# Two decode layers on one core: gate and up sums turned by VectorE, two query pieces ahead of the first query

## The chip, the cores and the metric

The kernel runs on one core of one Trainium2 chip. The metric is the device time of one execution in microseconds (us), lower is better; it was run three times. A separate execution was profiled. Engines are named TensorE (PE; its weight loads are listed apart as PEld), VectorE (DVE), ScalarE (ACT), GpSimd (POOL) and SyncE (SP), which here only issues DMA transfers.

## The reference

One token for each of two batch rows goes through attention, a gated feed-forward, the same attention and the same feed-forward again, with the same weights and the same caches both times:

```python
def _A_ref(x, k_cache, v_cache, wq, wo):          # x (2,1,576), caches (2,32,8192,128)
    q = (x @ wq).reshape(B, Sq, H, Dh).transpose(0, 2, 1, 3)
    scores = jnp.einsum("bhqd,bhkd->bhqk", q, k_cache) * (Dh ** -0.5)
    p = _softmax(scores, axis=-1)
    o = jnp.einsum("bhqk,bhkd->bhqd", p, v_cache)
    return o.transpose(0, 2, 1, 3).reshape(B, Sq, H * Dh) @ wo

def _B_ref(x, w_gate, w_up, w_down):              # 576 -> 4608 -> 576
    h = _gelu(x @ w_gate) * (x @ w_up)
    return h @ w_down

x = A_x
x = x + _A_ref(_layernorm(x), ...)
x = x + _B_ref(_layernorm(x), ...)
x = x + _A_ref(_layernorm(x), ...)
x = x + _B_ref(_layernorm(x), ...)
```

Everything is float32. The caches together are 537 MB and are read twice, less some pieces that are kept on the chip.

## The kernel before

**Space.** One SBUF tile, `space`, holds everything that comes from HBM: 49,920 floats in each partition. The class `Space` keeps a hand-written list of transfers in the order in which SyncE issues them. Each has a place, fixed or taken from a ring, and goes out when the place is free: `done(key)` after the last use of a piece frees its place, and `pump` issues what then fits. SyncE issues strictly in this order, so a transfer that waits for its place holds up all behind it. In the end the wait is on the reads of just those columns that the new transfer overwrites. Attention's key and value pieces use three large places of eight parts (a part is 2048 floats in each partition). Everything between the two attentions (output weights, the first feed-forward's weights, the second attention's query weights) goes through one ring, `mid`, of 6912 floats in each partition.

**Attention** (`attention`). The work is cut into items: a batch row with two heads (30 of them) or, for the last two heads, with one (4). For each item VectorE multiplies the keys by the query (L529), GpSimd adds halves of the products (L533), VectorE sums the rest (L539), then come a maximum (L550, a transposition on TensorE L552, L557), the exponent on ScalarE, and the values' products on TensorE (L601). The second attention takes the items backwards and starts with keys that stayed in SBUF. Its query weights arrive in pieces named `("wq", 1, half, i, s)`; `first_of_queries` multiplies those of the second half of the heads into `acc[1]`, `rest_of_queries` those of the first half into `xps`, and both stand on TensorE behind the first query (`query(0)`, L501), since the first items need only the tail of the query weights (`("wq", 1, "t")`).

**The normalization.** The sums are made from the raw x, beside a third column that sums the weights themselves; `norm` then makes `rstd` and `shift`, and a 6-row sum becomes the normalized result when its rows are weighted with `rstd` and `shift`. `pick`, `spread` and `chosen` are these weights, laid out so that a product on TensorE applies them: `chosen` in `query`, `spread` in `turned`.

**Feed-forward** (`mlp`). Gate and up sums of one half of the 4608 columns are collected in two PSUM banks (`products`, L719), 6 rows in each group of 32 partitions: three for gate, three for up. They have to get from rows to columns, since the down product needs the hidden values along the partitions. `copy` takes the banks to SBUF (`o`; ScalarE L729, VectorE L730), `turned` makes the columns with small products on TensorE that apply `spread` at the same time (L749 in layer 0: 72 for each half; L740 in layer 1: 18 for each half), and `gelu` works on the result (L758 to L764). A float32 product shows as two rows in the profile. `lower` multiplies with a piece of the down weights (L771); a quarter t of the rows uses half t // 2. In layer 0, `turned(0)` and `gelu(0)` stand among the products of the second half, and `turned(1)` and `gelu(1)` behind the first piece of the down weights. In layer 1, both halves are turned after the last up product.

Of the kernel before, what the change touches and what calls it, by code (L numbers as in the profile page):

```python
# [9 lines left out]
F32 = mybir.dt.float32  # L10
# [5 lines left out]
P = 128  # L16
# [81 lines left out]
def decode_layers(ctx, tc, x_in, kc, vc, wq, wo, wg, wu, wd, out):  # L98
# [202 lines left out]
    for c in range(4):  # L301
# [18 lines left out]
    pick = consts.tile([P, 4, 2, RW], F32, name="pick")  # L320
    nc.vector.tensor_copy(
        pick.rearrange("p c g r -> p c (g r)"), ident.rearrange("p (c x) -> p c x", c=4)[:, :, 0:WIN]
    )
# [27 lines left out]
    spread = consts.tile([P, 8, B], F32, name="spread")  # L351
# [39 lines left out]
    def norm(apart):  # L391
# [4 lines left out]
        for b in range(B):  # L396
# [3 lines left out]
        rstd = work.tile([P, B], F32, name="rstd")  # L400
        nc.gpsimd.tensor_tensor(out=rstd, in0=ve, in1=mhalf, op=ALU.pow)  # L401
        shift = work.tile([P, B], F32, name="shift")
        nc.vector.scalar_tensor_tensor(shift, mv[:, :, 0], -1.0, rstd, op0=ALU.mult, op1=ALU.mult)
        k8 = pick.rearrange("p c g r -> p (c g) r")
        part = work.tile([P, 8, B], F32, name="part")
        nc.vector.tensor_mul(spread, k8[:, :, 0:B], rstd.unsqueeze(1).to_broadcast([P, 8, B]))
        nc.vector.tensor_mul(
            part, k8[:, :, B:RW].to_broadcast([P, 8, B]), shift.unsqueeze(1).to_broadcast([P, 8, B])
        )
        nc.vector.tensor_add(spread, spread, part)  # L410
        nc.vector.reduce_sum(
            chosen.rearrange("p g b -> p (g b)"), spread.rearrange("p (c g) b -> p (g b) c", c=4), axis=AX.X
        )
# [9 lines left out]
    def attention(layer, items, apart):  # L423
# [35 lines left out]

        def first_of_queries():  # L460
            for i in range(NW):
                for s in range(2):
                    queries(
                        acc[1], window(1, i), at_of["wq", 1, 1, i, s], i == s == 0, False, s, range(4 - s)
                    )
                    done(("wq", 1, 1, i, s))
# [181 lines left out]

        query(0)
# [61 lines left out]
    def mlp(layer, apart):  # L711
# [3 lines left out]
        def products(half, s, lhs, at, stop):  # L715
            for c in range(4):
                key = half, s, c
                lo = at + (c * CF + s * BF if layer else c * BF)
                nc.tensor.matmul(  # L719
                    banks[half][s][32 * c:32 * c + WIN, 0:BF], lhs, space[:, lo:lo + BF],  # L720
                    start=key not in done_first, stop=stop,
                )
                done_first.add(key)

        o, gu, ga, hT = {}, {}, {}, {}

        def copy(half):
            t = o[half] = once.tile([P, 2, BF], F32, name="o", tag="row")
            nc.scalar.activation(t[:, 0, :], banks[half][0][:, 0:BF], AF.Copy)  # L729
            nc.vector.tensor_copy(t[:, 1, :], banks[half][1][:, 0:BF])  # L730

        def turned(half):
            t = o[half]
            gu[half] = psum2.tile([P, NI, 2, 2, B], F32, name="gu", tag="small")
            if layer:
                t = t.rearrange("p s w -> p (s w)")
                sel = spread.rearrange("p (c e g) b -> p e c g b", c=2, e=2)
                for i in range(NI):
                    for e in range(2):
                        nc.tensor.matmul(  # L740
                            gu[half][HALF * e:HALF * e + HALF, i, :, :, :], t[:, i::NI], sel[:, e, :, :, :],
                            start=True, stop=True,
                        )
                return
            sel = spread.rearrange("p (c g) b -> p c g b", c=4)
            for s in range(2):
                for i in range(NI):
                    for c in range(4):
                        nc.tensor.matmul(  # L749
                            gu[half][32 * c:32 * c + 32, i, s, :, :], t[:, s, i::NI], sel[:, c, :, :],  # L750
                            start=True, stop=True,
                        )

        def gelu(half):
            g = once.tile([P, NI, 2, B], F32, name="g")
            a = once.tile([P, NI, 2, B], F32, name="a")
            hT[half] = work.tile([P, NI, 2, B], F32, name="hT")
            nc.vector.tensor_copy(g, gu[half][:, :, :, 0, :])  # L758
# [5 lines left out]
            nc.vector.scalar_tensor_tensor(hT[half], a, 0.5, gu[half][:, :, :, 1, :], op0=ALU.mult, op1=ALU.mult)  # L764

        def lower(t, lo, hi):
            at = at_of["d", layer, t, lo]
            for i in range(lo, hi):
                for c in range(4):
                    a = at + (i - lo) * D + c * CW  # L770
                    nc.tensor.matmul(  # L771
                        xps[32 * c:32 * c + B, 0:CW], hT[t // 2][:, i, t % 2, :], space[:, a:a + CW],
# [4 lines left out]
        if layer == 0:  # L777
            for half in range(2):
                for g, name in enumerate("gu"):
                    for i in range(NW):  # L780
# [12 lines left out]
                copy(half)  # L793
            d = downs[0]
            lower(*d[0])
            turned(1)
            gelu(1)
            for piece in d[1:]:
                lower(*piece)
        else:  # L800
            def several(name, g, off, n):
                for u in range(off, off + n):
                    at = at_of[name, 1, off] + (u - off) * HF
                    for s in range(2):
                        products(u % 2, s, window(g, u // 2), at, u >= 6 and g == 1)
# [5 lines left out]
            for half in range(2):  # L811
                for s in range(2):
                    products(half, s, both, at_of["m", 1, half], False)
# [46 lines left out]
```

## Time and profile before

| | |
|---|---|
| median of 3 runs | 2699.47 us (2699.2 to 2701.33) |
| profiled execution | 2698.3 us, of which the span of the instructions 2696.5 us |
| instructions | 19594 |
| busy: PE, DVE, POOL, ACT | 952.5 (35%), 1870.6 (69%), 1171.5 (43%), 93.5 (3%) us |
| moved by DMA | 1154.45 MB, mean 428 GB/s |

How to read the lines further down. In a timeline a row is a run of instructions of one line: start in us, length in us, engine, line, operation, output<-inputs, shapes, count, and in brackets how long the engine stood before it and what released it. In a table of stretches a row is the stretch, its length, the busy time of PE, PEld, DVE, ACT and POOL with counts, the granted TensorE clock as a share of full speed, the mean busy share of the 16 DMA engines, and GB/s. In groups a row ends with busy us, mean ns of one | idle us before them. A DMA issue stands under SPq; its length is that of the issue and not of the transfer.

### The profile page before, as it was taken

To read this page: it belongs to the slowest core of one execution; us is meant where nothing else is said; L and a number is where in the kernel's file an instruction comes from. 1 tells how busy PE (TensorE), PEld (TensorE's weight loads), DVE (VectorE), ACT (ScalarE), POOL (GpSimd) and SP (SyncE) were. 2 spreads that over 40 slices of the span, in tenths; PEclk is the share of its full clock that TensorE was granted. 3 is DMA by queue.
4 is the path that set the end of the run, shared out by engine and by line. 5 is a ranking of instruction groups with operands and counts; after the bars stand their busy time and mean duration, and the time that the engine had idled before them with its cause. 6 is when DMAs were issued, how large, how long until landed. Compare 5 with 4: busy or idle time off the path is not lost.

```text
span 2696.5 us, 19594 instructions
## 1 busy us (share of the span) xinstructions
PE 952.5 (35%) x8132; PEld 343.0 (13%) x8132; DVE 1870.6 (69%) x1330; ACT 93.5 (3%) x421; POOL 1171.5 (43%) x342
## 2 busy tenths in 40 slices
PE   1332332233233323335664233233223322332346
PEld 0110111011111100112121011011101110110023
DVE  4678777877777777787048777877687778667750
ACT  0000000000000000000000000000000000000000
POOL 2445444544554455454025544544454445445530
PEclk7656665666566566656676665666566656665677
DMA  9999999999999999999999999999999999999998
GB/s 420 434 434 433 435 428 435 434 431 435 432 429 435 431 435 435 432 428 411 410 365 435 432 435 434 433 433 430 434 434 432 434 435 431 432 430 435 433 426 375
DMA packets 37226, 1154.45 MB, mean 428 GB/s; under 512 B 4225, under 2 KB 4881, under 8 KB 16145
## 3 DMA queue, kind: packets, MB, share of 16 engines
q1 hardware_dynamic: 37112, 1153.19, 99.6%
q8 instruction: 64, 1.05, 0.2%
q14 instruction: 26, 0.20, 0.0%
q10 hardware_dynamic: 24, 0.01, 0.0%
HBM read 1153.18 MB, written 0.00 MB: 428 GB/s over the span
## 4 chain that ended last, share of the span: by engine, by line
DMA 20%; DVE 15%; PE 9%; POOL 7%; issue 4%; ACT 1%; POOLq 0%; DVEq 0%; SPq 0%
DMA space<-in_A_k_cache_dram 17%; DVE space L529 9%; POOL space L533 7%; PE acc L601 6%; DVE S L539 5%; DMA space<-in_B_w_down_dram 2%; DMA space<-in_B_w_up_dram 1%; DVE osb L617 1%; PE nb L560 1%; ACT prz L572 1%; DMA space<-in_A_wq_dram 1%; PE xps L640 0%; PE tot L582 0%; DMA space<-in_A_wo_dram 0%; PE mT L552 0%
## 5 line engine op out<-in xcount | busy, mean ns | idle before, releaser
L533 POOL TENSOR_TENSOR space<-space 128x2048 f32<-128x2048 f32 (+1 forms) x332 | 1168.0, 3526 | 1302.3 <-DVE space L529 1025.7
L529 DVE TENSOR_TENSOR space<-space,qp 128x4096 f32<-128x4096 f32 (+1 forms) x332 | 1136.0, 3437 | 465.7 <-DMA space<-in_A_k_cache_dram 465.0
L539 DVE TENSOR_REDUCE S<-space 128x32 f32<-128x2048 f32 (+1 forms) x332 | 595.6, 1794 | 115.8 <-POOL space L533 112.9
L601 PE MATMUL acc<-space,prz 128*8 128x512 f32 x4096 | 590.4, 739 | 0.6 <-DMA space<-in_A_v_cache_dram 0.6
L625 PE MATMUL po<-weights,osb 128*32 128x1 f32 x1024 | 59.6, 201 | 1145.2 <-DVE osb L617 1145.2
L625 PEld LDWEIGHTS po<-weights,osb 128*32 128x32 f32 x1024 | 54.1, 154 | 1163.3 <-DVE osb L617 1163.1
L552 PE MATMUL mT<-ident,m 128*1 128x128 f32 x68 | 25.2, 370 | 406.6 <-DVE m L550 406.6
L601 PEld LDWEIGHTS acc<-space,prz 128*8 128x8 f32 x4096 | 112.4, 103 | 413.4 <-issue 409.7
L630 ACT COPY oT<-po 64x4 f32<-64x4 f32 (+1 forms) x68 | 10.7, 157 | 1905.0 <-PE po L625 1905.0
L617 DVE SCALAR_TENSOR_TENSOR osb<-acc,diag,osb 128x128 f32<-128x128 f32 x204 | 71.6, 351 | 7.2
L401 POOL TENSOR_TENSOR rstd<-ve,mhalf 128x2 f32<-128x2 f32 x4 | 2.8, 698 | 162.8 <-DVE ve L399 162.8
L560 PE MATMUL nb<-m,strip 1*128 1x1 f32 x256 | 64.7, 351 | 22.7 <-DVE m L557 22.7
L560 PEld LDWEIGHTS nb<-m,strip 1*128 1x128 f32 x256 | 58.9, 314 | 41.2 <-DVE m L557 41.1
L582 PE MATMUL tot<-rs,strip 128*128 128x2 f32 x120 | 34.9, 361 | 77.3 <-ACT prz L572 77.3
L552 PEld LDWEIGHTS mT<-ident,m 128*1 128x1 f32 x68 | 5.4, 79 | 418.6 <-DVE m L550 371.8
L572 ACT ACTIVATE prz<-S,nbs 64x128 f32<-64x128 f32 (+1 forms) x136 | 53.3, 392 | 3.3 <-ACT nbs L568 0.2
L557 DVE TENSOR_REDUCE m<-mT 1x2 f32<-1x128 f32 (+1 forms) x68 | 18.9, 278 | 34.3 <-PE mT L552 34.3
L582 PEld LDWEIGHTS tot<-rs,strip 128*128 128x128 f32 x120 | 29.8, 308 | 82.5 <-ACT prz L572 82.5
L719 PE MATMUL acc<-space,xt 128*6 128x288 f32 x256 | 30.4, 592 | 27.2 <-DMA space<-in_B_w_up_dram 14.9
L730 DVE COPY o<-acc 128x288 f32<-128x288 f32 x2 | 0.9, 458 | 52.4 <-PE acc L719 52.4
L615 DVE TENSOR_SCALAR osb<-acc,diag 128x128 f32<-128x128 f32 x68 | 23.3, 342 | 19.1 <-PE acc L601 19.1
L771 PE MATMUL xps<-space,hT 128*2 128x144 f32 x576 | 28.3, 356 | 13.6 <-DMA space<-in_B_w_down_dram 11.5
(93 smaller groups left out, 329.8 us busy)
## 6 DMA issues: line engine op xcount, KB each, us to landing
space<-in_A_k_cache_dram SPq DMA_DIRECT2D x6, 4096.0 KB, 21.4
space<-in_A_v_cache_dram SPq DMA_DIRECT2D x3, 4096.0 KB, 27.2
space<-in_B_w_gate_dram SPq DMA_DIRECT2D x18, 576.0 KB, 8.1
space<-in_B_w_up_dram SPq DMA_DIRECT2D x18, 576.0 KB, 7.8
space<-in_A_wo_dram SPq DMA_DIRECT2D x16, 576.0 KB, 7.1
space<-in_A_wo_dram SPq DMA_DIRECT2D x8, 1152.0 KB, 29.0
space<-in_B_w_gate_dram SPq DMA_DIRECT2D x2, 4608.0 KB
space<-in_B_w_down_dram SPq DMA_DIRECT2D x3, 2592.0 KB, 44.0
```

Of the source, the lines that this page charges most:

```text
L529: nc.vector.tensor_tensor(out=u, in0=t, in1=qp[n % 2][:, 0:DH].unsqueeze(1).to_broadcast([P, j, DH]), op=ALU.mult)
L533: nc.gpsimd.tensor_tensor(out=half, in0=half, in1=u[:, :, DH // 2:], op=ALU.add)
L539: nc.vector.tensor_reduce(out=S[n][:, 16 * lo:16 * hi], in_=half, axis=AX.X, op=ALU.add)
L552: nc.tensor.transpose(peaks[n], m, ident)
L560: nc.tensor.matmul(low[n], one_of[e] if heads == 2 else ones[0:1, :], m1[:, e:e + 1], start=(e == 0), stop=(e == heads - 1),)
L572: nc.scalar.activation(prz[rows_, n % 2, 0:item.rows // 4, e, :], s[rows_, 0:item.rows].rearrange("p (g r) -> p g r", r=4), AF.Exp, bias=n ...
L582: nc.tensor.matmul(tot, ones, rs[:, n % 2, :], start=True, stop=True)
L601: nc.tensor.matmul(acc[n % 2][32 * c:32 * c + 8, :], prz[:, n % 2, g, :, :].rearrange("p e r -> p (e r)"), space[:, at:at + 4 * DH], start ...
L617: nc.vector.scalar_tensor_tensor(t, q[:, r, :], diag[:, r:r + 1], t, op0=ALU.mult, op1=ALU.add)
L625: nc.tensor.matmul(po[lo + 32 * e:lo + 32 * e + 32, n % 2, i:i + 1], t[:, i::GH], w[:, e:e + 1], start=True, stop=True,)
L719: nc.tensor.matmul(banks[half][s][32 * c:32 * c + WIN, 0:BF], lhs, space[:, lo:lo + BF], start=key not in done_first, stop=stop,)
L771: nc.tensor.matmul(xps[32 * c:32 * c + B, 0:CW], hT[t // 2][:, i, t % 2, :], space[:, a:a + CW], start=(t == 0 and i == 0), stop=(t == NT ...
```

## The change

1. `copy`, `turned` and `gelu` become `hidden`. VectorE turns each PSUM bank in 32x32 blocks straight into SBUF (`nc.vector.transpose`, 128x288, read in steps of nine columns), and three further VectorE operations apply `rstd` and `shift`. The turning products, the ScalarE copies and `spread` are gone; `rstd` and `shift` become lasting tiles. `hidden(half)` stands directly behind the half's last sum in both layers, and all `lower` follow.
2. `chosen` is made directly, in three VectorE operations in place of four, from a smaller `pick`.
3. In the second attention the first two pieces of the query weights (`body(0)`, 7 products) are multiplied ahead of `query(0)`.
4. In layer 1 the columns of a half are cut in another order between the two banks, with the same number of products. The four output transfers are dealt differently to the two queues, still two for each.

The order and the waits of all transfers into SBUF stay the same.

```diff
-    pick = consts.tile([P, 4, 2, RW], F32, name="pick")
-    nc.vector.tensor_copy(...)
+    pick = consts.tile([P, 2, RW], F32, name="pick")
+    nc.vector.reduce_sum(pick.rearrange("p g r -> p (g r)"), blocks[:, 0:WIN, :], axis=AX.X)
...
-        nc.vector.tensor_mul(spread, k8[:, :, 0:B], rstd.unsqueeze(1).to_broadcast([P, 8, B]))
...
-        nc.vector.tensor_add(spread, spread, part)
-        nc.vector.reduce_sum(
-            chosen.rearrange("p g b -> p (g b)"), spread.rearrange("p (c g) b -> p (g b) c", c=4), axis=AX.X
-        )
+        nc.vector.tensor_mul(chosen, pick[:, :, 0:B], rstd.unsqueeze(1).to_broadcast([P, 2, B]))
...
+        nc.vector.tensor_add(chosen, chosen, part)
...
+        def body(i):
+            for s in range(2):
+                queries(acc[1], window(1, i), at_of["wq", 1, 1, i, s], i == s == 0, False, s, range(4 - s))
+                done(("wq", 1, 1, i, s))
+
         def first_of_queries():
-            for i in range(NW):
-                for s in range(2):
...
+            for i in range(1, NW):
+                body(i)
...
+        if layer == 1:
+            body(0)
         query(0)
...
-                lo = at + (c * CF + s * BF if layer else c * BF)
+                lo = at + c * BF
...
+        def hidden(half):
+            t = once.tile([P, 2, NI, 32], F32, name="turned", tag="row")
             for s in range(2):
...
+                nc.vector.transpose(t[:, s, :, :], banks[half][s][:, 0:BF].rearrange("p (j k) -> p k j", k=NI))
+            rows_ = t.rearrange("p s k w -> p (s k) w")[:, :, 0:WIN].rearrange("p t (g r) -> p t g r", g=2)
+            shape = [P, 2 * NI, 2, B]
+            gu = once.tile(shape, F32, name="gu")
+            part = once.tile(shape, F32, name="gupart")
+            nc.vector.tensor_mul(gu, rows_[:, :, :, 0:B], rstd.unsqueeze(1).unsqueeze(1).to_broadcast(shape))
+            nc.vector.tensor_mul(
+                part, rows_[:, :, :, B:RW].to_broadcast(shape), shift.unsqueeze(1).unsqueeze(1).to_broadcast(shape)
+            )
+            nc.vector.tensor_add(gu, gu, part)
+            g, u = gu[:, :, 0, :], gu[:, :, 1, :]
...
-                        if half == 1 and g == i == 0:
-                            turned(0)
-                            gelu(0)
...
-                copy(half)
-            d = downs[0]
-            lower(*d[0])
-            turned(1)
-            gelu(1)
-            for piece in d[1:]:
-                lower(*piece)
+                hidden(half)
...
             for half in range(2):
-                copy(half)
-                turned(half)
-                gelu(half)
-            for piece in downs[1]:
-                lower(*piece)
+                hidden(half)
+        for piece in downs[layer]:
+            lower(*piece)
```

More of the change, by code (lines that the diff above doesn't have):

```diff
@@ L723, in products @@
                 done_first.add(key)
[L725 to L745, printed above, removed]
-            for s in range(2):
[L747 to L752, printed above, removed]
@@ L812, in mlp @@
                 for s in range(2):
-                    products(half, s, both, at_of["m", 1, half], False)
+                    products(half, s, both, at_of["m", 1, half] + s * CF * 2, False)
                 done(("m", 1, half))
```

40 lines of the change are left out of this document (15 added, 25 removed).

## The prediction

> **What bounds the kernel now.** I read the page first, for the busy shares and the transfer rate along the span.
>
> ```profile
> span 2696.5 us, 19594 instructions
> ...
> DMA  9999999999999999999999999999999999999998
> GB/s 420 434 434 433 435 428 435 434 431 435 432 429 435 431 435 435 432 428 411 410 365 435 432 435 434 433 433 430 434 434 432 434 435 431 432 430 435 433 426 375
> ...
> q8 instruction: 64, 1.05, 0.2%
> ```
>
> No compute engine is over 69%, the DMA engines are full in nearly every slice, and the rate stands at 428 to 435 GB/s except around slices 19 to 21 and at the end. A slice is 2696.5 / 40 = 67.4 us, so the dip lies at about 1213 to 1415 us: the output weights, the first feed-forward layer and the query weights of the second attention, which all go through one small ring of SBUF. So I asked for the rate by stretches.
>
> ```profile
> 20.00:1180.00 1160.00, 360.87 (x2685) 124.41 (x2681) 840.33 (x526) 38.40 (x174) 532.12 (x147) 0.61 1.00 433
> ...
> 1300.00:1340.00 40.00, 27.26 (x372) 5.90 (x368) 2.03 (x10) 0.64 (x2) 0.00 (x0) 0.74 1.02 411
> 1340.00:1353.00 13.00, 10.33 (x234) 4.68 (x230) 1.62 (x7) 0.64 (x2) 0.00 (x0) 0.53 1.02 408
> 1353.00:1364.00 11.00, 4.73 (x93) 2.67 (x91) 0.00 (x0) 0.00 (x0) 0.00 (x0) 0.78 0.82 276
> 1364.00:1373.00 9.00, 6.62 (x108) 3.01 (x112) 0.00 (x0) 0.00 (x0) 0.00 (x0) 0.53 1.02 417
> 1373.00:1383.00 10.00, 7.25 (x77) 2.77 (x70) 4.47 (x18) 0.38 (x1) 0.69 (x1) 0.84 1.00 365
> 1383.00:1392.00 9.00, 5.49 (x69) 1.79 (x62) 8.71 (x6) 0.00 (x0) 6.68 (x3) 0.88 0.84 269
> 1392.00:1490.00 98.00, 52.26 (x347) 17.56 (x341) 78.68 (x70) 6.45 (x30) 49.28 (x19) 0.67 1.02 431
> 1490.00:2600.00 1110.00, 345.14 (x2552) 119.82 (x2552) 827.63 (x521) 36.81 (x169) 525.80 (x144) 0.61 1.00 433
> ```
>
> The last three columns are the granted TensorE clock, the DMA share and GB/s. Transfers are the bound: both long attention stretches run at 433 GB/s with a DMA share of 1.00. The engines go short in two places only, at 1353 to 1364 (share 0.82, 276 GB/s) and at 1383 to 1392 (0.84, 269 GB/s). A microsecond of transfer won there moves everything behind it, because 1392 to 2600 has no hole to swallow it.
>
> What the holes cost: the first has the layer's gate and up rate of 411 GB/s as its measure, 11 x (1 - 276/411) = 3.6 us. The second has as measures the 365 just ahead of it, with many small rows, giving 9 x (1 - 269/365) = 2.4 us, and 411, giving 3.1 us; I take the middle, 2.7. Together 6.3 us, bounds 6.0 to 6.7.
>
> **First hole: the products that turn the sums.** TensorE around it, then SyncE's issues of the down weights, with their row of the table of transfers as the last line (count, KB each, median us from issue to landing):
>
> ```profile
> 1345.34 1.15 PE L719 MATMUL qp<-space,xm 128*6 128x288 f32 x8 [0.27 <-DMA space<-in_B_w_up_dram]
> 1347.45 1.62 PE L771 MATMUL xps<-space,hT 128*2 128x144 f32 x24 [0.97 <-DMA space<-in_B_w_down_dram]
> 1348.85 2.39 PE L749 MATMUL gu<-spread,o 128*32 128x4 f32 x144
> 1351.08 2.10 PE L771 MATMUL xps<-space,hT 128*2 128x144 f32 x30
> 1355.14 3.88 PE L771 MATMUL xps<-space,hT 128*2 128x144 f32 x74 [1.97 <-issue]
> 1360.44 0.67 PE L771 MATMUL xps<-space,hT 128*2 128x144 f32 x16 [1.42 <-DMA space<-in_B_w_down_dram]
> ```
>
> ```profile
> 1349.13 0.33 SPq L189 DMA_DIRECT2D space<-in_B_w_down_dram  x1
> ...
> 1352.28 0.33 SPq L189 DMA_DIRECT2D space<-in_B_w_down_dram  x1
> ...
> 1355.81 0.33 SPq L189 DMA_DIRECT2D space<-in_B_w_down_dram  x1
> ...
> space<-in_B_w_down_dram SPq DMA_DIRECT2D x12, 576.0 KB, 7.4
> ```
>
> The first down piece is multiplied at 1347.45, then 144 turning products (L749) hold TensorE for 2.39 us, and then it stands 1.97 us with "issue" as its releaser. The ring holds 6912 floats a partition, 3.54 MB, or 8.6 us at 411 GB/s; a piece takes 7.4 us from issue to landing and some 1.15 us of TensorE. The loop of 8.55 us has no room for a delay of 2.39 + 1.97 = 4.4 us. The issues show it: after 1349.13 the next two, which need the second and third piece's room, come at 1352.28 and 1355.81.
>
> Afterwards the products are gone from TensorE (the order of its instructions shows the down products in one unbroken run of 144), and VectorE does two block turns from PSUM and three small operations instead. The down products of the first two quarters need only the first half's result, long ready, so TensorE takes the second piece at 1347.45 + 1.62 = 1349.1 and the third by about 1350.3. The two issues then come at about 1350.2 and 1351.4, 2 and 4.4 us earlier, which is before the engines run dry. The stretch 1364 to 1373 is the same loop without turning products: 417 GB/s. So the hole closes: **-3.6 us**, bounds -2.0 (if the "issue" wait stays, below) and -3.6. The first half's products (another 144) delayed no transfer: 1300 to 1340 is at 411. They count nothing.
>
> **What VectorE's new work costs.** The nearest rows:
>
> ```profile
> L373 DVE STREAM_TRANSPOSE xt<-x 128x128 f32<-128x128 f32 x4 | 1.6, 405 | 0.1
> ...
> L385 DVE STREAM_TRANSPOSE xtm<-x 128x32 f32<-128x32 f32 x4 | 0.9, 235 | 0.1
> ...
> L730 DVE COPY o<-qp 128x288 f32<-128x288 f32 x2 | 0.9, 454 | 19.9 <-PE qp L719 19.9
> ...
> L759 DVE TENSOR_TENSOR a<-g 128x36 f32<-128x36 f32 x4 | 0.8, 196 | 0.1
> ```
>
> Four blocks take 405 ns and one 235, so a block adds 57 ns and nine would take 235 + 8 x 57 = 0.69 us from SBUF. No row shows a block turn out of PSUM, with steps of nine elements at that. The 454 ns of the copy is its lower end, twice 0.69 = 1.4 us my upper one; I take 0.7, since the copy shows that reading PSUM isn't slow. A half is then 2 x 0.7 + 3 x 0.25 + 6 remaining operations at 0.2 with short gaps, about 1.4 us: some 3.5 us. In layer 0 the second half's chain starts at 1345.34 + 1.15 = 1346.5 and ends near 1350, and the third quarter of the down weights lands only about 10 us later. So it is hidden; its cover is gone only if a turn takes over 4 us. The removed ScalarE copies and the shorter scale chain (one operation fewer, 0.2 us) lie beside waits for transfers and count nothing.
>
> **Second hole: the pieces ahead of the first query.**
>
> ```profile
> 1379.26 0.59 PE L436 MATMUL xps<-space,xm 128*6 128x256 f32 x2
> 1381.27 0.78 PE L501 MATMUL qp<-qsb,chosen 6*64 6x128 f32 x8 [1.41 <-DVE chosen L411]
> 1381.97 5.40 PE L436 MATMUL acc<-space,xt 128*6 128x256 f32 x56
> 1390.80 0.62 PE L436 MATMUL acc<-space,xm 128*6 128x256 f32 x8 [3.43 <-DMA space<-in_A_wq_dram]
> ```
>
> ```profile
> 1379.88 0.54 SPq L148 DMA_DIRECT2D space<-in_A_wq_dram  x1
> ...
> 1383.06 0.54 SPq L148 DMA_DIRECT2D space<-in_A_wq_dram  x1
> ...
> 1383.91 1.26 SPq L170 DMA_DIRECT2D space<-in_A_wq_dram  x1
> ```
>
> TensorE is idle from 1379.85 to 1381.27, waiting for VectorE's `chosen`, and only after the query does it begin the waiting pieces. SyncE's issues at 1383.06 and 1383.91 need just the room of the first two. The change puts those two, 7 matmuls shown as 14 rows, into the idle: 14 x 5.40/56 = 1.35 us against 1.41 us of idle. The query slips by at most 0.2 us and the two issues come at about 1380.5 and 1381.1, 2.6 and 2.8 us earlier; the following ones wait on the next pieces, which TensorE reaches about 1.3 us earlier, and on SyncE, which no longer starts late. The transfers then have over 2 us queued at each issue. **-2.7 us**, bounds -1.3 (only TensorE's shift counts) and -3.1. What is queued behind the two pieces on TensorE is the first query and all of VectorE's first item; they lose 0.2 us, but VectorE has far more idle soon after:
>
> ```profile
> 1402.06 1.02 PE L436 MATMUL xps<-space,xt 128*6 128x256 f32 x8 [0.62 <-DMA space<-in_A_wq_dram]
> ...
> 1403.41 0.28 DVE L557 TENSOR_REDUCE m<-mT 1x1 f32<-1x128 f32 x1 [5.46 <-PE mT L552]
> ```
>
> VectorE stands 5.46 us until TensorE has finished the query weights, whose last piece lands just before 1402.06. When that comes 2.7 us earlier, VectorE resumes 2.7 us earlier too, so its item work does not become the limit. SyncE's list of transfers, and its order, are the same in both kernels.
>
> **The end of the kernel.**
>
> ```profile
> 2670.45 0.46 DVE L730 COPY o<-acc 128x288 f32<-128x288 f32 x1 [32.42 <-PE acc L719]
> ...
> 2678.88 6.16 PE L771 MATMUL xps<-space,hT 128*2 128x144 f32 x144
> ...
> 2686.99 2.39 PE L771 MATMUL xps<-space,hT 128*2 128x144 f32 x72 [1.94 <-DMA space<-in_B_w_down_dram]
> ...
> 2692.39 1.16 PE L771 MATMUL xps<-space,hT 128*2 128x144 f32 x32 [0.68 <-DMA space<-in_B_w_down_dram]
> ```
>
> TensorE waits for down weights at 2686.99 and at 2692.39, so the 72 turning products here, and their end 8 us before, are covered: 0 us. The new chain of both halves needs about 7 us from 2670 and must be done by 2687. The output's regrouped transfers are again two per queue: 0. Startup: one reduction in place of a copy, while the first weights load: 0.
>
> **Sum.** 3.6 + 2.7 = 6.3 us, less 0.3 for a wait that I may have missed in either loop: 6.0 us. The profiled execution took 2698.3 us (span 2696.5 and 1.8 around it), 1.2 below the median of 2699.47; I take the difference off the median: **2693.5 us**.
>
> **The rivals.**
> A. The "issue" wait is not the burst's. I read the 1.97 us as TensorE short of instructions: 144 products with their weight loads, 288 instructions, went by in 2.4 us, and the next were not there. If it has another cause it stays, and only 3.6 x 2.39/4.36 = 2.0 us of the first hole close: 2.0 + 2.7 - 0.3 = 4.4, 2695.1 us. For it: the profile names no cause. Against it: it occurs right behind the burst and not again in the down products. [...]
> B. The second attention is paced by VectorE. Then the query weights land early but the caches' room is freed no sooner than VectorE's start allows, and the second gain is lost: 3.3 us, 2696.2. For it: VectorE works without a break for a while from 1403.41. Against it: the 5.46 us ahead of that.
> C. The holes are filled and reappear, since the slots of the caches fix the later issues: 2699. Against it: 431 and 433 GB/s right behind.
> D. Slower: the block turns out of PSUM are dear. In the last layer the chain of four turns and two times 2.1 us starts at 2669.5 and must end by 2686.9, so it decides from (17.4 - 4.2)/4 = 3.3 us a turn, and each further us costs 4 at the end. At 6.5 us, 9 times my estimate, it costs 12.8 against 6.0: 2706.3. For it: no row shows the form. Against it: PSUM copies of the same size take 0.45.
>
> **How the numbers follow.** Measurement of this kernel can tell about 0.2%, 5.4 us. The forecast has 0.66, of which 0.56 gain over 5.4 us and 0.10 less; A 0.12, B 0.09, C 0.06 lie within 0.2%; D 0.07, of which 0.05 is slower by over 0.2%. So faster 0.56, same 0.39, slower 0.05. The range runs from 2692.0 (both holes at their full bound of 6.7 give 2692.8, and the runs scatter by about 1 us) to 2696.5 (B, likewise), leaving out C, D and the tails, under 2 in 10.
>
> **What would show it.** Right: the rate at what was 1353 to 1364 is near 411 and at 1383 to 1392 above 350; no "issue" wait behind the first down piece; the issue after the second down piece about 1 us behind the one before; the turns near 0.7 us; the wait for the peak (L557 before) shorter than 5.46 us by no more than the second gain; the stream from there on at 431 to 433 and ending about 6 us earlier. Wrong: a DMA share under 0.9 in either stretch, a new dip in the 100 us behind, or a final down product that waits for VectorE.

## The result, and the profile after

The changed kernel takes 2694.3 us (median of 17 runs, 2691.65 to 2696.5), the one before 2699.2 us (17 runs, 2696.45 to 2701.59): 4.9 us less, a ratio of 0.9984 (95% interval 0.9976 to 0.9991). The forecast was 2693.5 us and 6.0 us less. The gain is clear of the noise, but at 0.16% it stays under the 0.2% (5.4 us) that the prediction thought likelier than not. The profiled execution took 2694.77 us, span 2692.9.

Of the page of after, the span, the rate by slices and the queue of instructions:

```profile
span 2692.9 us, 18872 instructions
...
GB/s 421 435 434 435 427 436 429 436 434 433 431 435 434 435 429 436 429 431 413 407 385 440 431 434 432 433 432 434 432 434 431 435 433 433 432 435 431 432 427 379
...
q8 instruction: 61, 1.00, 0.1%
```

Slice 21 went from 365 to 385 GB/s; the other slices differ by at most 8. The queue of instructions (q8) brought 61 packets, where it was 64. The same stretches as before (granted clock, DMA share and GB/s at the end of a row):

```profile
1340.00:1353.00 13.00, 9.83 (x112) 2.47 (x104) 2.54 (x10) 0.23 (x1) 0.00 (x0) 0.54 1.01 386
1353.00:1364.00 11.00, 6.07 (x120) 2.79 (x112) 0.00 (x0) 0.00 (x0) 0.00 (x0) 0.77 1.00 397
1364.00:1373.00 9.00, 5.50 (x100) 2.29 (x100) 0.00 (x0) 0.00 (x0) 0.00 (x0) 0.69 1.03 403
1373.00:1383.00 10.00, 8.64 (x73) 3.27 (x68) 4.57 (x17) 0.38 (x1) 0.69 (x1) 0.68 0.81 292
1383.00:1392.00 9.00, 6.05 (x65) 1.47 (x58) 8.72 (x6) 0.65 (x2) 7.00 (x3) 0.81 1.00 378
1392.00:1490.00 98.00, 52.15 (x319) 17.12 (x319) 82.43 (x72) 5.80 (x28) 49.47 (x20) 0.64 1.02 433
1490.00:2600.00 1110.00, 347.18 (x2617) 123.49 (x2621) 826.79 (x521) 36.97 (x170) 526.36 (x145) 0.61 1.00 432
```

The first hole is closed: 397 in place of 276 GB/s. Where the second was there are 378 in place of 269. But a new hole stands directly ahead of it: 1373 to 1383 was at 365 with a share of 1.00, and is at 292 with 0.81. The stretch behind is as fast as before.

TensorE at the first hole, and SyncE's issues of the down weights:

```profile
1346.22 1.14 PE L715 MATMUL qp<-space,xm 128*6 128x288 f32 x8 [0.26 <-DMA space<-in_B_w_up_dram]
1348.34 2.58 PE L751 MATMUL xps<-space,hT 128*2 128x144 f32 x40 [0.97 <-DVE gupart L732]
1351.07 1.12 PE L751 MATMUL xps<-space,hT 128*2 128x144 f32 x16 [0.16 <-DMA space<-in_B_w_down_dram]
1352.48 0.67 PE L751 MATMUL xps<-space,hT 128*2 128x144 f32 x16 [0.28 <-DMA space<-in_B_w_down_dram]
```

```profile
1349.06 0.33 SPq L189 DMA_DIRECT2D space<-in_B_w_down_dram  x1
1350.02 0.33 SPq L189 DMA_DIRECT2D space<-in_B_w_down_dram  x1
1350.98 0.33 SPq L189 DMA_DIRECT2D space<-in_B_w_down_dram  x1
```

The wait called "issue" is gone; from the second piece on TensorE waits for transfers only. The issue after the second piece comes 0.96 us behind the one ahead of it, where it was 3.15. (The releaser of the first wait, `gupart`, had begun only 0.25 us earlier and is nothing that the product reads. In before the same wait, also 0.97 us, is put down to the transfer of the weights.)

VectorE's new work, the end of the second half's chain, and the wait for the peak:

```profile
1347.42 0.48 DVE L726 STREAM_TRANSPOSE turned<-qp 128x288 f32<-128x288 f32 x1 [0.92 <-PE qp L715]
1347.94 0.23 DVE L731 TENSOR_TENSOR gu<-turned,rstd 128x72 f32<-128x72 f32 x1
...
1349.79 0.20 DVE L744 SCALAR_TENSOR_TENSOR hT<-a,gu 128x36 f32<-128x36 f32 x1
...
1400.06 0.28 DVE L551 TENSOR_REDUCE m<-mT 1x1 f32<-1x128 f32 x1 [2.44 <-PE mT L546]
```

A block turn takes 0.48 us and the chain is done at 1349.99. TensorE at the second hole, and SyncE's first issue of a query piece that needs the room of the tails:

```profile
1374.58 3.58 PE L429 MATMUL acc<-space,xt 128*6 128x256 f32 x8 [0.87 <-DVE xt L372]
1378.09 0.66 PE L393 MATMUL every<-apart,strip 128*128 128x48 f32 x2
...
1380.95 0.65 PE L495 MATMUL qp<-qsb,chosen 6*64 6x128 f32 x8 [0.49 <-DVE chosen L406]
1381.53 1.91 PE L429 MATMUL acc<-space,xt 128*6 128x256 f32 x28
...
1386.13 1.03 PE L429 MATMUL acc<-space,xt 128*6 128x256 f32 x6 [1.36 <-DMA space<-in_A_wq_dram]
```

```profile
1380.06 1.18 SPq L148 DMA_DIRECT2D space<-in_A_wq_dram  x2
1381.34 1.39 SPq L170 DMA_DIRECT2D space<-in_A_wq_dram  x2
```

The two pieces stand ahead of the query, as meant, and the query is issued 0.32 us earlier than before. But the first row of TensorE is new: the eight rows of the tail's products (four products, `("wq", 1, "t")`) reach over 3.58 us, where the same row of before reads 1.89. (The expectations below call the rows products and give the two cases as 2.9 and 1.5 us.) The issue at 1380.06 needs the room that these and the next few products give back. The tail's first product came 2.07 us earlier than before (1374.58 for 1376.65), and yet this issue comes 0.18 us later (before: 1379.88). By then the queue was running empty. What stretched the products is the granted clock:

```profile
1365.73:1369.14 3.41, 1.52 (x40) 0.76 (x40) 0.00 (x0) 0.00 (x0) 0.00 (x0) 1.00 1.01 416
1369.14:1379.38 10.24, 8.22 (x66) 2.87 (x67) 2.47 (x12) 0.00 (x0) 0.00 (x0) 0.50 1.02 381
1379.38:1382.80 3.42, 2.93 (x44) 1.35 (x42) 1.90 (x6) 0.38 (x1) 0.69 (x1) 1.00 0.45 119
```

These are stretches between steps of the clock: the clock stands at half while the tail is multiplied, and the transfers run dry right behind (119 GB/s). In before's execution the same products ran at full:

```profile
1364.57:1374.80 10.23, 7.70 (x116) 2.91 (x108) 0.00 (x0) 0.00 (x0) 0.00 (x0) 0.50 1.02 406
1374.80:1381.65 6.85, 4.26 (x38) 1.92 (x38) 3.20 (x17) 0.38 (x1) 0.69 (x1) 1.00 1.00 367
```

**Two lengths for the comparison.** Fixed stretches slide against the work when a kernel becomes faster. So I added up the bytes that SyncE's queue moved, in the order of its issues, and read off when the last gate or up piece, the last down piece and the last query piece were through. D is the time from the first to the second (10.6 MB), Q from the second to the third (9.4 MB). What follows Q belongs to both kernels alike: to the last transfer ahead of the long stream 124.4 to 124.9 us, and from there to the end 1170.4 to 1172.2 us in all fourteen profiles. In the table "mean" is the mean of all timed runs less the mean of before's runs beside them, in us, with a 95% interval from the scatter of single runs; "clock" is that at the four tail products, rounded (in e2, e3 and e11 it stepped up before their end).

| kernel | D | Q | clock | mean against before |
|---|---|---|---|---|
| before | 29.55 | 27.30 | 1.0 | |
| before, second profile (e11) | 29.05 | 27.65 | 0.5 | -1.1 ± 1.0 |
| changed | 26.95 | 26.80 | 0.5 | -4.4 ± 1.0 |
| changed, second profile (e5) | 26.05 | 28.30 | 0.5 | -4.6 ± 1.2 |
| turn alone (e1) | 26.25 | 27.65 | 0.5 | -3.2 ± 0.9 |
| queries alone (e2) | 29.30 | 25.50 | 0.5 | -1.6 ± 0.8 |
| burst of short products back (e3) | 28.65 | 25.65 | 0.5 | -2.6 ± 1.0 |
| few long products (e4) | 27.75 | 26.80 | 0.5 | -4.0 ± 1.0 |
| norm behind the tail (e6) | 27.60 | 28.70 | 0.5 | -4.2 ± 1.4 |
| clock kept up (e7) | 26.10 | 24.40 | 1.0 | -6.0 ± 1.1 |
| e7 and at the end (e8) | 27.25 | 25.85 | 1.0 | -4.6 ± 1.0 |
| e8 and norm behind the tail (e9) | 26.75 | 25.90 | 1.0 | -5.4 ± 1.0 |
| e7 without the queries ahead (e10) | 29.40 | 26.75 | 1.0 | -4.6 ± 1.0 |
| clock up from the fourth piece (e12) | 27.10 | 25.15 | 1.0 | -6.3 ± 1.0 |

The row of e11 is the measure of trust: the kernel of before against itself gave -1.1 by this mean (ratio 0.9996, 0.9987 to 1.0005). Differences of about 1 us are therefore not shown by times. e1 to e4, e5 to e7, e8 to e10, and e11 with e12 were one batch each.

D and Q belong to the one execution that was profiled: its time less D and Q is 2640.6 to 2642.2 us in all fourteen. That execution is not always a typical one. In e10 it is the slowest of the eleven (2697.46 us, median 2694.51), in e6 the second slowest (2697.21, median 2695.0), in e7 the second fastest (2691.72, median 2693.3). So the long D of e10, the long Q of e6 and the short Q of e7 are partly the luck of the execution.

### The profile page after: what moved, and what is told of

The parts are those of the page before. It is cut to its first block, busy times and chain, and to the rows that moved or that the text cites. A ratio compares the mean times of both kernels' runs of the same rounds, so it can differ in the third digit from the quotient of the medians.

```text
span 2692.9 us, 18872 instructions
## 1 busy us (share of the span) xinstructions
PE 950.3 (35%) x7772; PEld 333.9 (12%) x7772; DVE 1873.1 (70%) x1338; ACT 92.0 (3%) x417; POOL 1171.4 (43%) x342
## 4 chain that ended last, share of the span: by engine, by line
DMA 23%; DVE 15%; PE 8%; POOL 7%; ACT 1%; issue 1%; SPq 0%; POOLq 0%; DVEq 0%
DMA space<-in_A_k_cache_dram 17%; DVE space L523 9%; POOL space L527 7%; PE acc L595 6%; DVE S L533 5%; DMA space<-in_B_w_down_dram 3%; DMA space<-in_B_w_up_dram 2%; DVE osb L611 1%; PE nb L554 1%; ACT prz L566 1%; DMA space<-in_B_w_gate_dram 1%; DMA space<-in_A_wq_dram 1%; PE xps L634 0%; PE tot L576 0%; DMA space<-in_A_wo_dram 0%
```

## The experiments

**The parts.** The theory: the turned sums close the first hole, the pieces ahead of the query the second.

e1, the change without the pieces ahead of the query:

```diff
-            for i in range(1, NW):
+            for i in range(NW):
                 body(i)
...
-        if layer == 1:
-            body(0)
         query(0)
```

> The turn by VectorE alone; all query pieces again behind the first query. Theory: the two parts add up. The first hole stays closed (about 397 GB/s where before had 276, no wait of 2 us with the releaser 'issue' behind the first down piece), and the hole at the query weights comes back at 2.5 to 3 us wherever the clock stands. Gain over before 2.5 to 3.6 us, so 2695.6 to 2696.7. Rival: the query pieces moved ahead caused the shortage of 0.81 that the changed kernel shows at 1373 to 1383; then it is gone here, and the gain is at least the changed kernel's, 4.9 us or more.

2696.53 us against 2699.2, ratio 0.9988 (0.9979 to 0.9997).

```profile
1353.00:1364.00 11.00, 7.40 (x120) 3.25 (x124) 0.00 (x0) 0.00 (x0) 0.00 (x0) 0.58 1.02 412
1373.00:1383.00 10.00, 8.42 (x61) 3.35 (x64) 5.35 (x18) 0.38 (x1) 0.73 (x2) 0.71 0.80 281
```

The time lies in the 2695.6 to 2696.7 expected. The first hole closes, and the new one (share 0.80) is there as well: the moved pieces did not bring it. At 1383 to 1392 the rate is 352 GB/s, so the second hole did not come back in its old place; the shortage now lies ahead of it.

e2, the kernel of before with `body(0)` ahead of `query(0)`:

> The kernel before with two query pieces ahead of the first query, and nothing else. Theory: the first hole stays at 276 GB/s, and the second closes as far as TensorE's clock allows: 1.5 to 2.7 us gained, 2696.5 to 2697.7. Rival: the second part brings nothing by itself, since the transfers are short of room for the tail of the query weights and not for these pieces: no difference, within 0.5 us.

2697.98 us, ratio 0.9994 (0.9985 to 1.0003): by itself not told from no change, and by the medians a little less than the 1.5 expected; by the mean -1.6 ± 0.8. Q is 25.5, and the first hole with its "issue" wait stays, as TensorE's timeline of e2 shows:

```profile
1349.58 2.39 PE L752 MATMUL gu<-spread,o 128*32 128x4 f32 x144
...
1355.78 4.55 PE L774 MATMUL xps<-space,hT 128*2 128x144 f32 x74 [1.87 <-issue]
```

The two parts add up: 3.2 + 1.6 = 4.8 us against 4.4 to 4.6 for both.

**What the burst of short products costs.** Both kernels are the changed one with needless products on constants behind the first down piece, into room that nothing reads:

```diff
+        def idle_work(n, rows, cols):
+            t = psum2.tile([P, 256], F32, name="unused", tag="small")
+            for k in range(n):
+                nc.tensor.matmul(t[32 * (k % 4):32 * (k % 4) + rows, 0:cols], ident[:, 0:rows], strip[:, 0:cols], ...)
...
         for n, piece in enumerate(downs[layer]):
             lower(*piece)
+            if layer == 0 and n == 0:
+                idle_work(72, 32, 4)     # e3; in e4 idle_work(9, 32, 256)
```

> The changed kernel with 72 needless products of 4 columns on TensorE at the place of the turning products of the first layer's second half (constants as operands, results not used; nothing waits for VectorE). Theory: the products alone made the first hole. TensorE runs 144 rows in about 2.4 us, then stands about 2 us with the releaser 'issue', and the hole of 3 us or more is back: about 3 us slower than the changed kernel, near 2697.5. Rival: what made the hole was the wait for VectorE's and ScalarE's copies; then nothing changes against the changed kernel.

> The changed kernel with 9 needless products of 256 columns at the same place: 18 rows in place of 144, about the same 2.3 us at half clock (1.2 at full). Theory: half of the hole came from the number of instructions. Then there is no 'issue' wait behind them, and at most half of the hole (0 to 1.8 us) is back: 2694.3 to 2696. Rival: TensorE's time alone matters; then the hole is as large as with the short products and the 'issue' wait is there too.

e3, TensorE's timeline:

```profile
1349.61 2.10 PE L760 MATMUL unused<-strip,ident 128*32 128x4 f32 x144
...
1356.20 2.12 PE L751 MATMUL xps<-space,hT 128*2 128x144 f32 x58 [1.59 <-issue]
```

e4, the same place:

```profile
1349.26 2.34 PE L760 MATMUL unused<-strip,ident 128*32 128x256 f32 x17
...
1351.82 2.18 PE L751 MATMUL xps<-space,hT 128*2 128x144 f32 x42
1354.70 0.92 PE L751 MATMUL xps<-space,hT 128*2 128x144 f32 x24 [0.71 <-DMA space<-in_B_w_down_dram]
```

e3 took 2696.37 us (0.999, 0.9982 to 0.9999), e4 2696.03 us (0.9986, 0.9977 to 0.9994). The many short products (2.10 us) bring the "issue" wait of 1.59 us back, the few long ones, which hold TensorE about as long (2.34 us for 17 of their 18 rows), do not. So here the wait belongs to the number of instructions (144 rows against 18), as the prediction had read it.

The traces also show when the packets of the queue of instructions came (q8; 64 of them with 1.05 MB in before, so 16 KB each). In each of the four profiles with this wait a packet is under way when the wait begins, and TensorE goes on 1.33 to 1.53 us after it is through: in before the packet runs from 1352.70 to 1353.61 and the wait from 1353.17 to 1355.14; the packets of e2, e3 and e11 end at 1354.45, 1354.71 and 1353.54. The next packet starts 3.5 to 4.7 us after the one before it there; in after and e4 no two start less than 11 us apart between 1340 and 1375. This fits the reading that TensorE has run out of instructions and waits for more; that the landing of the packet is what releases it was not tried by itself.

By time the burst costs less than the 3 us expected of e3: its mean gain is 2.6 us, where the changed kernel has 4.4 and 4.6, and it is 1.4 ± 1.1 us behind e4. e4 itself is not told from the changed kernel. D is 28.65 and 27.75 against 26.05 and 26.95 in the two profiles of the changed kernel: 1.7 to 2.6 us more for the short burst, 0.8 to 1.7 more for the same time in long products. The latter is hardly above what D reaches without either (27.6 in e6, and 29.4 in the slow execution of e10).

**The new hole.** e5 is the changed kernel as it is.

> The changed kernel, with nothing altered. If the half clock at the eight products of the query-weight tail belongs to this kernel, the second profile shows them over about 2.9 us again and moves 290 GB/s or so from 1373 to 1383 us; time 2694.3 us. If the clock there was an accident of that one execution, the eight take 1.5 us, the stretch from the first query transfer to the last lasts about 24.4 us in place of 26.8, and the profiled execution is 2 us or more shorter.

```profile
1373.00:1383.00 10.00, 9.06 (x72) 3.21 (x64) 5.01 (x17) 0.38 (x1) 0.69 (x1) 0.66 0.77 254
```

```profile
1374.15 3.58 PE L429 MATMUL acc<-space,xt 128*6 128x256 f32 x8 [0.87 <-DVE xt L372]
```

2695.0 us (0.9983, 0.9973 to 0.9992). The same 3.58 us, and a deeper hole. e6 moves one call:

```diff
             done(("wq", 1, "t"))
-            norm(apart)
...
             done(("wq", 1, "tm"))
+            norm(apart)
```

> The changed kernel with the sums for the second norm issued behind the products of both tails in place of between them: the two products `every`, which take 0.66 us and wait for VectorE's xm, no longer stand ahead of the products that give the room of the tails back. Theory (the hole from 1379 us on ends when that room comes back): the first query piece that waits for it is issued 0.6 us earlier or somewhat more, and the time falls by 0.4 to 0.6 us, to 2693.8; the chain to `chosen` starts 0.6 us later, which VectorE's idle time there covers. Rival (the hole is set by the chain to `chosen` and what stands behind it, not by that room): no gain, or 0.6 us slower.

2695.0 us (0.9985, 0.9977 to 0.9994), the same as e5 in the same batch. From the end of the down pieces to the issue that needs the tail's room it was 10.1 us, against 10.2 in e5 and 9.4 in the first profile: the 0.6 us did not show, so this run gives the theory no support. It doesn't bear out the rival either; at half clock all around, the executions scatter by more than that. (e9 below makes the same move at full clock.)

e7 holds the clock up:

```diff
         for n, piece in enumerate(downs[layer]):
             lower(*piece)
+            if layer == 0 and n >= 8:
+                idle_work(2, 32, 256)
```

> The changed kernel with two needless products of 256 columns on constants, into room that nothing reads, behind each of the last eight down pieces of the first layer, so that TensorE has more to do before the tails come. Theory (the clock falls to half because TensorE has too little to do there, and the eight tail products then take 2.9 in place of 1.5 us, so that their room comes back late): the clock stays at 1.0, the eight take 1.5 to 1.7 us, the first piece that needs their room is issued 1.5 to 2.5 us earlier, and the time falls by 1.5 to 2.4 us, to 2692 to 2692.8. Rival (the hole comes from the order of the transfers, and the clock only accompanies it; or the clock does not follow the work that TensorE has): 2694.3 us, or up to 1 us more, since the needless products stand in the way of down products at half clock.

```profile
1373.00:1383.00 10.00, 6.93 (x72) 2.30 (x69) 7.07 (x16) 0.38 (x1) 3.77 (x3) 1.00 0.99 374
1383.00:1392.00 9.00, 5.42 (x70) 1.34 (x74) 9.00 (x6) 0.65 (x2) 6.33 (x3) 0.99 1.03 412
```

```profile
1372.64 1.89 PE L429 MATMUL acc<-space,xt 128*6 128x256 f32 x8 [0.45 <-DVE xt L372]
```

2693.3 us (0.9978, 0.9969 to 0.9987). With more work for TensorE its clock is at 1.00 and 0.99 in the two stretches (0.66 and 0.81 in e5), the tail's products are back at 1.89 us, and both stretches run without a hole. Q is 24.4, that is 2.9 under before, about the prediction's 2.7, in an execution that was faster than most. By the medians e7 is 1.7 us under e5 of the same batch, though the intervals overlap and the 2693.3 lies above the 2692 to 2692.8 expected.

What the clock does to the tail can be read without the times, as the stretch from the tail's first product to the issue that needs its room (the one at 1380.06 in after). With `norm` in its place it is 3.23 or 3.24 us in all five executions with the clock at full (before, e7, e8, e10, e12), and 4.6 to 5.9 us in all seven with it at half or mostly at half (after 5.48, e5 5.90, e1 5.57, e2 4.79, e3 4.59, e4 5.37, e11 4.67). The kernel of before is on both sides.

e8 adds the same at the end of the second layer (8 ahead of the first down piece, 16 behind each of the first two), e9 to that e6's edit, e10 takes the moved pieces out of e7.

> The kernel of the run before (needless products behind the last eight down pieces of the first layer) with the same at the end of the second layer: 8 needless products of 256 columns ahead of the first down piece there and 16 behind each of the first two. Without them the last 144 rows of products in that place took 7.5 us at a clock of 0.5 and were the end of the chain of waits. Theory (a TensorE that waits much is clocked at half, and pays for it where the end of its work sets the time): those products take about 4 us, and the time falls by 2 to 4 us below the kernel without these, to 2689.5 to 2691.5. Rival (needless products at half clock hold the down products up more than the clock gives back): 2693 to 2697.

> As the kernel with needless products in both layers, and the sums for the second norm behind the products of both tails. At full clock the two products `every` take 0.35 to 0.4 us: if the room of the tails sets the rest of the hole, the first query piece that waits for it is issued that much earlier and the time falls by 0.3 us; if nothing is left to win there, as the transfer rate of 374 GB/s from 1373 to 1383 us suggests for at least the half of it, no change that these runs can tell.

> Needless products behind the last eight down pieces of the first layer, and the two pieces of query weights not multiplied ahead of the first query. With the clock held at full, this shows what the pieces moved ahead are worth by themselves. By the prediction's working 2.7 us (bounds 1.3 to 3.1): from the last down piece to the last query piece 27.1 us in place of 24.4, and 2.7 us slower than with them, 2696. If the moved pieces were never worth more than the 0.5 us that the changed kernel showed: 24.9 us, 2693.8.

e8 took 2694.84 us (0.9982, 0.9973 to 0.9991): no gain over e7, where 2 to 4 us were expected. Its last products, with the clock at 1.00 from 2668.33 to 2685.40, where e7 has 0.50:

```profile
2683.24 2.39 PE L751 MATMUL xps<-space,hT 128*2 128x144 f32 x72 [2.21 <-DMA space<-in_B_w_down_dram]
2686.52 1.41 PE L751 MATMUL xps<-space,hT 128*2 128x144 f32 x40 [0.90 <-DMA space<-in_B_w_down_dram]
2688.62 1.16 PE L751 MATMUL xps<-space,hT 128*2 128x144 f32 x32 [0.69 <-DMA space<-in_B_w_down_dram]
```

Each still waits for its transfer. The 7.5 us in one run of rows that I had taken for the bound mostly filled the time until the last weights came. In e7 the last product ended 1.82 us after the last packet of weights, in e8 0.95 us after it, as in ten other profiles (0.92 to 0.95; e1 and e3 have 1.42 and 1.56). So the most that a full clock could give there is, as an estimate from 1.82 less 0.95, about 0.9 us, and not 2 to 4.

e9: 2693.96 us (0.9981, 0.9972 to 0.999), not told from e8. But the move did what it should: from the tail's first product to the issue that needs its room it took 2.78 us, where e8 has 3.24. That is 0.46 us, near the 0.35 to 0.4 expected; its worth in time is too small for these runs.

e10: 2694.51 us (0.998, 0.9971 to 0.9989). Its Q of 26.75 is near the 27.1 expected of 2.7 us for the moved pieces, while its mean gain of 4.6 is that of e8 and 1.4 us short of e7's, nearer the other expectation. Its D of 29.4 is out of line: TensorE waited long for down weights there, with no needless product yet issued. It is the profile of the slowest run, and what made that run slow in this place stays open:

```profile
1356.33 2.58 PE L749 MATMUL xps<-space,hT 128*2 128x144 f32 x40 [3.11 <-DMA space<-in_B_w_down_dram]
...
1364.23 1.62 PE L749 MATMUL xps<-space,hT 128*2 128x144 f32 x24 [2.92 <-DMA space<-in_B_w_down_dram]
```

The last two, the kernel of before and e7 with the needless products from the fourth piece on (`n >= 3`):

> The kernel of before, with nothing altered: a second profile of it, to see how far the two lengths on which the argument rests differ between executions. From the last gate or up piece to the last down piece it was 29.55 us, from there to the last query piece 27.3 us, with the eight tail products at full clock in 1.5 us. If these belong to the kernel, both come back within 0.5 us, with the wait put down as issue behind the burst. If the clock at the tail is a matter of the execution, the eight take 2.9 us here and the second length is 1.5 to 2.5 us more. By time: no difference.

> The changed kernel with two needless products of 256 columns behind each down piece of the first layer from the fourth on, in place of the last eight, so that any delay that they bring at half clock is over well before the tails. Theory (the clock at the tail costs time, and the needless products in themselves a little): clock 1.0 through the tail, the two lengths together no more than the 50.5 to 53.1 us of the kernels with eight or nine such pieces, time 5.5 to 6 us under before. Rival (what the needless products cost at half clock grows with their number): 4 us under before or less, no better than the changed kernel.

e11, 2699.3 us against 2700.1:

```profile
1349.04 2.39 PE L749 MATMUL gu<-spread,o 128*32 128x4 f32 x144
...
1354.89 4.51 PE L771 MATMUL xps<-space,hT 128*2 128x144 f32 x74 [1.53 <-issue]
...
1376.35 3.33 PE L436 MATMUL acc<-space,xt 128*6 128x256 f32 x8 [0.87 <-DVE xt L373]
```

The first hole comes back with its "issue" wait. But now the tail's products run mostly at half clock here too (3.33 us for the eight rows, where the first profile has 1.89), so the clock is a matter of the execution and not of the change. Q is only 0.35 us longer for it (27.65), where 1.5 to 2.5 were expected, though the issue that needs the room of the first query piece came 1.2 us later than in the first profile (1384.28 for 1383.06). Why Q grew by so little stays open. e12 took 2693.98 us against 2700.1 (0.9977, 0.9968 to 0.9986), with the clock at 1.0 throughout the tail; time and lengths came about as its theory expected.

e7 and e12 are the fastest versions measured, at 0.9978 and 0.9977 of before, where the changed kernel is at 0.9984 and 0.9983. The four versions with queries ahead and the clock up average 1.1 ± 0.9 us under the two sets of the changed kernel. Given e11, that is likely and not shown.

## Why the prediction was right, and where it was off

The measured 2694.3 us lies 0.8 us from the forecast of 2693.5. That it lies in the range of 2692.0 to 2696.5 decides little, since rivals A (2695.1) and B (2696.2) would lie there too. What decides between them is the traces.

**First hole, -3.6 (bounds -2.0 to -3.6): right in mechanism, somewhat too large.** D fell from 29.55 and 29.05 to 26.95 and 26.05, or 2.8 on the mean. Over the three profiles with the turning products and the nine with neither them nor a burst in their place, the means are 29.3 and 27.05, or 2.25 less. By times the turn alone is worth 3.2 ± 0.9. The issues came at 1350.02 and 1350.98 (forecast 1350.2 and 1351.4). In the profiled execution the full 411 GB/s was not reached (397, and 386 just ahead); in e1 it was (412).

**Rival A is refuted.** No "issue" wait is left in after, and e3 brings it back with a burst of another kind. The wait is 1.53 to 1.97 us in four profiles behind 144 rows of short products, and there is none behind nine long products. That the wait is one for instructions is supported by the packets of q8 (TensorE goes on 1.33 to 1.53 us after one is through) and was not shown by itself.

**VectorE's work and rival D.** A turn takes 0.48 us, at the lower end of the 0.454 to 1.4, and far from the 3.3 from which D would decide. The chain ended at 1349.99 and the third quarter of the down weights lies far behind it; off the path, as costed. At the end the last products still wait for transfers: 0 us, as said.

**Second hole, -2.7 (bounds -1.3 to -3.1): this is the mis-sized term.** Its step was "the two issues then come at about 1380.5 and 1381.1, 2.6 and 2.8 us earlier". They came at 1380.69 and 1381.34, near those times. But the forecast had read them off an execution without the first gain, and adding 3.6 and 2.7 asks for both on top of each other: with D shorter by 2.6 us the two issues should have come that much earlier still. What held them is the issue ahead of them, the one that needs the tail's room. The forecast took the time at which that room comes back from an execution in which the clock there stood at full; in after it was at half, and the 2.07 us by which the tail started earlier were lost by then. Q fell by 0.5 in the profiled execution of after, and rose in e5; over the six profiles with queries ahead at half clock it is 25.5 to 28.7, mean 27.0. With the clock at full it is 24.4 to 25.9 (four profiles, mean 25.3), against 27.3 and 26.75 without them: 1.7 less, within the bounds, and the 2.7 is reached in one profile only. At half clock the pieces are worth less: 27.0 against 27.65 without them (e1 and e11), or 0.7, under the lower bound. By times the moved pieces are worth 1.6 ± 0.8 on the kernel of before. The sum also took for granted that the stretch ahead, which it used only as a measure, stays as it was: the sign named as wrong for the two holes, a DMA share under 0.9, occurred between them, at 1373 to 1383 (0.81). What of the missing microsecond is clock and what is scatter stays open: the traces show the clock's effect on the tail plainly (1.89 against 3.25 to 3.58 us for the eight rows, and 1.4 to 2.7 us more until the room is back), the times do not separate it.

**Rivals B and C.** VectorE still waits for the query weights: 2.44 us, from 5.46. That is 3.0 shorter, more than the second gain alone, since the wait ended 3.35 us earlier (1400.06 for 1403.41), by both gains, while the query that starts VectorE's first item came only 0.32 us earlier. So VectorE was not the limit there. The stream behind is at 433 and 432, so neither a second attention paced by VectorE nor a hole behind is seen. A hole did come up again, but ahead.

**The sum.** The forecast of -6.0 was -3.6, -2.7 and +0.3. Measured: about -3 and -1.5 for the two parts, -4.9 for the whole by the medians. The 0.3 kept for a missed wait had the right sign; 6.3 less 4.9, or 1.4, was needed.

## What to carry to other kernels

Many tiny products in a row can cost more than their time on TensorE (here 2.1 to 2.4 us, and 1.5 to 2.0 us of wait behind them): count instructions as well as microseconds. If another engine can do the step in a few instructions off the path, the loop is rid of both. When transfers are the bound and a small ring feeds them, follow each issue back to the product that gives its room, and ask at which clock that product will run; a duration read from one execution can be another in the next (here 1.89 and 3.33 us for the same eight rows of the same kernel). Before explaining 1 us by a mechanism, profile the unchanged kernel a second time, and see where the profiled execution stands among the others.

## What was not expected of the hardware

In the traces of before and after the granted clock has two values, 0.5 and 1.0, and each of the 165 stretches from step to step in either trace is a whole multiple of 3.413 us (1 to 15 times). Stretches between steps near the end of e7:

```profile
2654.68:2661.50 6.82, 4.20 (x72) 1.59 (x68) 0.00 (x0) 0.00 (x0) 0.00 (x0) 1.00 1.02 433
2661.50:2664.92 3.42, 2.81 (x28) 0.70 (x16) 2.46 (x10) 0.23 (x1) 0.00 (x0) 0.50 0.96 412
2664.92:2668.33 3.41, 1.21 (x40) 1.08 (x44) 2.42 (x11) 0.23 (x1) 0.00 (x0) 1.00 1.02 438
2668.33:2685.40 17.07, 12.59 (x212) 7.32 (x205) 0.00 (x0) 0.00 (x0) 0.00 (x0) 0.50 0.80 337
```

Their lengths are 2, 1, 1 and 5 times 3.41 us. The same kernel had either clock at the same products (before: 1.0, and 1.89 us for the eight rows; e11: mostly 0.5, and 3.33 us); what sets the steps in an execution no run here shows. e7's theory, that the clock falls because TensorE has too little to do, does not cover the last row: TensorE is occupied for 12.59 of 17.07 us there (74%), mostly with products of two columns of weights (`128*2`), and the clock is at 0.50, while in the first row it is occupied for 4.20 of 6.82 us (62%) at 1.00. In the first layer two products with 32 columns of weights behind each of the last eight or nine pieces went with a full clock (0.98 to 1.00 from 1364 to 1392 in e7), and all five profiles with them have 1.0 at the tail, against one of nine without. Whether the columns of weights make the difference was not tried by itself.
